# An exponential's table loaded one slot earlier, a freer choice of slots for side work, and two sums issued with their product, in a kernel that runs TensorE from end to end

## The chip, the cores and the metric

The kernel runs on one core of a Trainium2 chip. The metric is device time in microseconds (us), the median over several executions. One execution is also recorded by the hardware profiler; the times inside it are counted from the start of its span.

## The reference

Two mixers of the same input `x` (2048 tokens of 1024) are blended token by token by a gate. `a` is attention with 32 heads of 32, in which every token looks at 8 tokens at distances 0, 2, ... 14; `b` is a gated MLP whose gate half is normalised and mixed along the sequence by the 2048 x 2048 matrix `w_sp`.

```
g   = sigmoid((x * gate_w).sum(-1))
qkv = x @ wqkv                                  # 1024 -> 3 x 1024, 32 heads
attn = softmax(q . k[pos - 2w] * scale), w = 0..7   # masked where pos - 2w < 0
a   = (attn . v[pos - 2w]) @ wo
z   = gelu(x @ w_in)                            # 1024 -> 2 x 1792
b   = (z1 * (w_sp @ layernorm(z2) + b_sp)) @ w_out
out = g * a + (1 - g) * b
```

## The kernel before

All products run on TensorE, most of them by a Strassen-like scheme: one block product is made of seven half-size products (`a11`, `s1`, `s2`, `a12`, `s3`, `s4`, `a22`) that share PSUM banks. A bank that has been read out by a copy is added to by later products, so a product into it has to wait for the copy. The scheme works with 16-bit floats, for which operands are scaled by powers of two; the powers come from sums of magnitudes that are taken beside the other work.

The stages, by the profile's clock: projections to z2 and to the first heads' q, k, v (to 92 us, with x turned round and scaled); projections of two groups of heads with z2's last columns in between, as eight **projection groups** (`z2_group`, 92 to 182 us); the last three groups of heads and the rest of z2 (to 270 us); z1 (to 362 us); the **mixing** along the sequence, sixteen groups (`g_group`, n = 0 to 15, 362 to 532 us); the product with wo; the product with w_out (580 us to the end).

The attention itself runs on VectorE beside all of this, from 92 to about 497 us: for each of eight groups of heads a product of q with k (L505), folds of it (L509, L512), the maximum and its subtraction (`soft_a`, L526 to L529), the exponential on ScalarE (L552), the sum and division (`soft_b`, L556 to L562), a product with v (L572) and its folds (L578, L579, L575).

Every engine runs its instructions in the order in which they are written. That order is made when the kernel is built, by a planner, `Beat`. It keeps a clock `beat.now` that advances by the columns of the matmuls as they are written (`beat.run`), a list of steps with due times (`beat.at`), and an estimate of when VectorE is free (`beat.vector`, pushed on by `on_vector`). Whenever `beat.run` advances, it writes all steps that have fallen due, the attention's among them. In the projection groups an attention step is written when its start is at most 0.3 us ahead, in the mixing at most 0.5.

In a projection group the products `s1`, `s3` and `s4` go to the banks `pd`, `pa` and `pd`, tiles of q, k, v (L938, copied out by ACT at L941) lie between, and two sums (L486, L487) put the group's last two blocks together on VectorE. The second of them reads the bank `pd`, which frees it.

A mixing group writes its seven products and, on ScalarE, in this order: a copy of `pa` into a second bank (the *fork*, L1130), a *fork slot* for side work, the copies `p5` (L1116) and `u2` (L1118), the first block's copy from `pb` (L1152), a *copy slot* for side work, the copy `u3` (L1118), two passes of magnitudes of the group before (L885), and the last block's copy (L1168). In every odd group from 3 on, both slots are taken by the scaling of an earlier unit (L903). In the others side work may take them, from two lists of steps with due times:

- `beside_fork`, for the fork slot, holds the pass over o's magnitudes (`o_norm_now`, L681, 1.9 us). What has not been done by the time VectorE is to write over `o`'s buffer is written there and then, by the attention's own product (`pv_steps`).
- `beside_copy`, for the copy slot, holds first a tiny exponential (L1193) that only makes the table be loaded, and then seven passes over chunks of A_wo (`wo_norm`, L858, 768 columns each). All chunks use one buffer: each pass, when it is written, plans the load of the next chunk (L854) for 1 us later.

ScalarE holds one table of functions at a time. The mixing's first exponential follows GELUs, so a table load precedes whichever exponential comes first. All loads and stores are issued by SyncE (SP), in one order.

Of the kernel before, what the change touches and what calls it, by code (L numbers as in the profile page):

```python
# [35 lines left out]
DN = ZC + 2  # L36
# [26 lines left out]
def kernel(  # L63
# [13 lines left out]
    nc = tc.nc  # L77
# [67 lines left out]
    wsc = sm.tile([P, 4], F32, name="wsc")  # L145
# [11 lines left out]
    cm05 = sm.tile([P, 8], F32, name="cm05")  # L157
# [22 lines left out]
    m11, m12, m21, m22 = [d_h[:, q] for q in range(4)]  # L180
# [159 lines left out]
    beat = Beat()  # L340
# [6 lines left out]
    TT = nc.vector.tensor_tensor  # L347
# [30 lines left out]
    def z2_out(src, i, c, scale):  # L378
        nc.scalar.activation(z2[:, i, ZC * c:ZC * (c + 1)], src, ACT.Gelu_apprx_tanh, scale=scale,
                             accum_out=s1[:, 4 * i + c:4 * i + c + 1])  # L380
# [61 lines left out]
    def z2_keep(ps):  # L442
        out = z2_snaps[z2_kept[0] % 5]
        z2_kept[0] += 1
        nc.scalar.copy(out, ps[:, 0:DN - 1])
        return out

    def z2_product(ps, w, v, first):
        for k in range(4):
            lhsT = w[:, k // 2, k % 2, :] if len(w.shape) == 4 else w[:, k, :]  # L450
            nc.tensor.matmul(ps[:, 0:DN - 1], lhsT, v[:, k, 0:DN - 1], start=(first and k == 0), stop=(k == 3),  # L451
                             skip_group_check=True)
        beat.run(4 * (DN - 1))

    def z2_late(i, src, scale):
        z2_out(src[:, 0:ZC], i, 3, scale)
        nc.scalar.activation(gl_s[:, i:i + 1], src[:, ZC:ZC + 1], ACT.Copy, scale=scale)
# [3 lines left out]
    def z2_group(u, tiles):  # L461
        v = tokens[u]
        scale = zinv
        pa, pd = [psum.tile([P, 512], F32, name="ps", tag="ps") for _ in range(2)]
        z2_product(pa, v.a11, m11, True)
        pb = seeded.tile([P, 512], F32, name="seed", tag="sd")
        nc.scalar.copy(pb[:, 0:DN - 1], pa[:, 0:DN - 1])
        tiles.pop(0)()
        z2_product(pd, v.s1, r1, True)
        p5 = z2_keep(pd)  # L470
        z2_product(pa, v.s2, r2, False)
        u2 = z2_keep(pa)
        tiles.pop(0)()
        while z2_wait:
            z2_late(*z2_wait.pop(0))
        z2_product(pb, v.a12, m21, False)
        z2_out(pb[:, 0:ZC], 2 * u, 2, scale)
        z2_product(pa, v.s3, r3, False)
        u3 = z2_keep(pa)
        tiles.pop(0)()  # L480
        prep["owed"] += 2 if 0 < u < 5 else 0
        some = release()
        if not some:
            square_owed(u)
        z2_product(pd, v.s4, m22, False)
        TT(p5, p5, u3, ALU.add)  # L486
        TT(u2, u2, pd[:, 0:DN - 1], ALU.add)  # L487
        beat.on_vector(1.3)
        z2_product(pa, v.a22, r4, False)
        z2_out(pa[:, 0:ZC], 2 * u + 1, 2, scale)  # L490
        tiles.pop(0)()
        if not release(True) and not some and u % 2 == 1:
            square_owed(u)
        z2_wait.extend([(2 * u + 1, p5, scale), (2 * u, u2, scale)])
# [44 lines left out]
    def release(last=False):  # L539
        for fn in list(held):  # L540
            if not (last and fn is exp_now):
                held.remove(fn)
                fn()
                return True
        return False
# [49 lines left out]
    def load_v(g):  # L595
        sync.dma_start(v_t, bass.AP(tensor=v_d.tensor, offset=v_d.offset + (g * (S + 16) + 2) * C, ap=[[NJ * C, P], [1, NJJ * C]]))
# [5 lines left out]
    def attention_steps(t):  # L602
        ready = t
        beat.at(t - 8.0, lambda: load_qk(0))
        beat.at(t - 7.9, lambda: load_v(0))
        for g in range(NG):
            if g == 1:
                t = max(t, ready + 28.0)
            for took, fn in qk_steps(0) + qk_steps(1):
                yield t, took, fn  # L610
            t = beat.vector
            if g + 1 < NG:
                beat.at(t + 1.0, lambda g=g: load_qk(g + 1))
            if g > 0:
                for took, fn in pv_steps(g - 1, 0):
                    yield t, took, fn
                t = beat.vector
            yield t + (0.5 if g == 0 else 0.0), 1.7, soft_a
            t = beat.vector
            exp_wait.append(g)  # L620
            beat.at(t + 1.0, lambda: hold_back(exp_now))
            if g == 0:
                t += 5.0
            else:
                for took, fn in pv_steps(g - 1, 1):
                    yield t, took, fn
                t = beat.vector
                beat.at(t + 1.0, lambda g=g: load_v(g))
                beat.at(t + 1.5, lambda g=g: store_o(g - 1))
                o_wait.append(lambda g=g: o_norm(g - 1, obuf))  # L630
                if prep["mixing"]:
                    beside_fork.append((t + 12.0, o_norm_now))
                else:
                    beat.at(t + 17.0, o_norm_soon)
            yield t, 2.3, lambda g=g: soft_b(g)
            t = beat.vector
        for took, fn in pv_steps(NG - 1, 0) + pv_steps(NG - 1, 1):
            yield t + 5.0, took, fn
        t = beat.vector
        beat.at(t + 1.0, attended)  # L640

    beside_fork, beside_copy, behind_mult = [], [], []
# [5 lines left out]
            room[0] -= behind_mult[0][1]  # L648
            behind_mult.pop(0)[2]()

    def spare(queue):
        if queue and queue[0][0] <= beat.now:
            queue.pop(0)[1]()

    def attended():
        store_o(NG - 1)
# [195 lines left out]
    def load_wo_chunk(m):  # L852
        n = min(768, 8192 - 768 * m)
        sync.dma_start(w_chunk[:, 0:n], wo_flat[:, 768 * m:768 * m + n])  # L854

    def wo_norm(m):
        n = min(768, 8192 - 768 * m)
        nc.scalar.activation(w_chunk[:, 0:n], w_chunk[:, 0:n], ACT.Abs, accum_out=l1[:, m:m + 1])  # L858
        if m < 10:
            beat.at(beat.now + 1.0, lambda: load_wo_chunk(m + 1))  # L860

    def w_total():
        nc.vector.memset(zeros[:], 1.0)
# [136 lines left out]
    def square_owed(u):  # L1000
        if prep["owed"] > 0:
            prep["owed"] -= 1
            squares(u)
            return True
# [35 lines left out]
    t = beat.now  # L1040
# [18 lines left out]
    t = beat.now  # L1059
# [4 lines left out]
    t = beat.now  # L1064
# [13 lines left out]
    for c in range(4):  # L1078
        w1 = w1_slots[c]
        for i in range(16):  # L1080
# [5 lines left out]
            ps = bank()  # L1086
# [46 lines left out]
    def g_group(n):  # L1133
        u, fb = n // 2, n % 2
        f0, f1 = fb * ZC, fb * ZC + ZC
        v = pairs[u % 2]
        lo, hi = [bt[:, 2 * u + h:2 * u + h + 1] for h in range(2)]
        g, z = g_ring[n % 4], z1_ring[n % 2]
        now(("z1", n), ("y", u - 2))
        pa, pd = [psum.tile([P, 512], F32, name="ps", tag="ps") for _ in range(2)]  # L1140
        product(pa, v.a11, b11, f0, f1, True)
        pb = fork(pa, ZC, lo)
        if n % 2 == 1 and n > 1:
            y_scale_beside((n - 3) // 2, 0)
        else:
            spare(beside_fork)
        product(pd, v.s1, t1, f0, f1, True)
        p5 = keep(pd, None)
        product(pa, v.s2, t2, f0, f1, False)
        u2 = keep(pa, lo)  # L1150
        product(pb, v.a12, b21, f0, f1, False)
        nc.scalar.copy(g[:, 0, 0], pb[:, 0:ZC])  # L1152
        if n % 2 == 1 and n > 1:
            y_scale_beside((n - 3) // 2, 1)
        else:
            spare(beside_copy)
        idle_vector()
        product(pa, v.s3, t3, f0, f1, False)
        u3 = keep(pa, hi)
        if n > 0:  # L1160
            y_norm(n - 1)
        vec(g[:, 1, 1], p5, u3)
        product(pd, v.s4, b22, f0, f1, False)
        vec(g[:, 0, 1], pd[:, 0:ZC], u2)
        if fb == 0 and n > 0:
            y_power(n // 2 - 1)
        product(pa, v.a22, t4, f0, f1, False)
        nc.scalar.activation(g[:, 1, 0], pa[:, 0:ZC], ACT.Identity, bias=hi)  # L1168
        TT(g, g, z, ALU.mult)
        beat.on_vector(1.1)  # L1170
        room[0] = 7.0 if fb == 1 else 6.5 if n == 14 else 1.5
        idle_vector()
        if n + 2 < 2 * NU:
            soon(("z1", n + 2), lambda: load_z1(n + 2))
# [15 lines left out]

    for n in range(2):
        load_z1(n)
    beside_copy.append((0.0, lambda: nc.scalar.activation(wsc[:, 3:4], cm05[:, 0:1], ACT.Exp)))  # L1193
    for m in range(4, 11):
        beside_copy.append((beat.now + 1.0, lambda m=m: wo_norm(m)))
    behind_mult.append((beat.now + 134.0, 0.5, w_total))
# [1 line left out]
    for n in range(2 * NU):  # L1198
        u, fb = n // 2, n % 2
        t = beat.now  # L1200
# [21 lines left out]
    t = beat.now  # L1222
# [110 lines left out]
    for u in range(NU):  # L1333
        v = rows[u % 5]
        lo, hi = [omr[:, 2 * u + h:2 * u + h + 1] for h in range(2)]
        m11, m12, m21, m22 = halves(u, mix)
        o11, o12, o21, o22 = halves(u, ob_slots)
        pa, pd = [psum.tile([P, 512], F32, name="ps", tag="ps") for _ in range(2)]
# [6 lines left out]
        p5 = hold(pd, hi)  # L1345
        product(pa, v.s2, e2, 0, 512, False)
        u2 = hold(pa, lo)
# [4 lines left out]
        u3 = hold(pa, hi)  # L1352
# [53 lines left out]
```

## Time and profile before

| What | us |
|---|---|
| median of 3 runs (672.32 to 672.66) | 672.64 |
| the profiled execution | 671.37 |
| its span | 669.6 |
| TensorE busy in the span | 663.5 |
| VectorE busy | 575.2 |
| ScalarE busy | 441.6 |
| DMA: moved, mean share of the 16 engines | 123.92 MB, 69.8% |
| mixing, 362 to 532: TensorE, VectorE, ScalarE busy of 170 | 169.25, 155.72, 120.05 |

In the profile PE is TensorE's matmuls, PEld its weight loads, DVE is VectorE, ACT ScalarE, SP the engine that issues the DMAs. Busy time counts an instruction from start to end. The ends of matmuls are modelled, so that gaps between matmuls are better read from their starts. A row of the timeline merges instructions of one kind that follow each other, and its bracket gives the idle time of the engine just before and what ended it. Idle time of an engine matters only where TensorE, or whatever runs last, waits for it.

### The profile page before, as it was taken

The page shows a single profiled execution, that of the slowest core. Times are in us where ns is not written, and L with a number is a line of the kernel's source. Part 1 is how long each engine was busy: PE and PEld are TensorE (multiplying, and loading weights), DVE is VectorE, ACT ScalarE, POOL GpSimd, SP SyncE. Part 2 cuts the span into 40 slices and gives each one's busy share as a digit, 9 for nine tenths or more (in the row PEclk, how much of TensorE's full clock was granted, in tenths as well). Part 3 has the DMA queues.
Part 4 walks back from the last instruction along what each step waited for, and adds up shares of the span by engine and source line. Part 5 has one row for each costly group of instructions (what it writes and reads, how often), then busy time and mean ns, then how long its engine had stood idle before and what let it go on. Part 6 is the DMA issues. An engine that isn't in the chain of part 4 may idle for free.

```text
span 669.6 us, 9598 instructions
## 1 busy us (share of the span) xinstructions
PE 663.5 (99%) x3564; PEld 389.8 (58%) x3564; DVE 575.2 (86%) x660; ACT 441.6 (66%) x774; POOL 9.4 (1%) x68
## 2 busy tenths in 40 slices
PE   9999999999999999999999999999999999999998
PEld 4568876666777777555555455555555544444443
DVE  4667999989999999999999999999978788954745
ACT  4437667788889989889754568777777774522122
POOL 0000000000001000000000000000000000000000
PEclk9999999999999999999999999999999999999999
DMA  8999574354298996994956686648589799476211
GB/s 237 176 246 269 103 203 131 91 121 119 49 278 250 281 303 186 277 342 146 276 209 217 140 216 162 159 123 231 141 209 287 144 242 253 93 159 150 56 63 64
DMA packets 229919, 123.92 MB, mean 185 GB/s; under 512 B 191088, under 2 KB 217456, under 8 KB 229872
## 3 DMA queue, kind: packets, MB, share of 16 engines
q1 hardware_dynamic: 229872, 123.31, 69.8%
q8 instruction: 28, 0.46, 0.3%
q14 instruction: 19, 0.16, 0.1%
HBM read 63.97 MB, written 37.82 MB: 152 GB/s over the span
## 4 chain that ended last, share of the span: by engine, by line
PE 55%; DVE 40%; ACT 3%; issue 2%; DVEq 0%; ACTq 0%
PE ps L1106 36%; DVE arena L509 8%; DVE arena L505 7%; DVE arena L572 7%; PE seed L1106 6%; PE ps L938 6%; DVE arena L578 3%; PE ps L370 2%; DVE arena L801 2%; PE sd L938 2%; DVE arena L579 2%; DVE arena L819 2%; DVE arena L575 1%; DVE att_L L512 1%; PE sd L370 1%
## 5 line engine op out<-in xcount | busy, mean ns | idle before, releaser
L1106 PE MATMUL ps<-arena 128*128 128x448 f16 (+1 forms) x1296 | 263.7, 363 | 0.7 <-ACT arena L1118 0.6
L1106 PEld LDWEIGHTS <-arena 128*128 128x128 f16 x1519 | 148.5, 98 | 155.0 <-issue 1.5
L938 PEld LDWEIGHTS <-arena 128*128 128x128 f16 (+1 forms) x1024 | 141.4, 138 | 30.6 <-issue 1.1
L938 PE MATMUL ps<-arena 128*128 128x384 bf16 x800 | 142.5, 326 | 0.7 <-DVE arena L487 0.7
L1089 PEld LDWEIGHTS <-arena 128*128 128x128 f16 x512 | 50.0, 98 | 46.6
L509 DVE TENSOR_TENSOR arena<-arena 128x4096 bf16<-128x4096 bf16 (+1 forms) x64 | 74.0, 1157 | 1.8
L1089 PE MATMUL ps<-arena 128*128 128x448 bf16 x384 | 75.4, 352 | 0.0
L505 DVE TENSOR_TENSOR arena<-arena 128x8192 bf16<-128x8192 bf16 x16 | 70.8, 4422 | 4.4 <-DMA arena<-k_d 4.1
L572 DVE TENSOR_TENSOR arena<-arena,att_A 128x8192 bf16<-128x8192 bf16 x16 | 70.7, 4420 | 0.2
L941 ACT CAST arena<-ps 128x384 bf16<-128x384 f32 x100 | 47.8, 487 | 29.4 <-PE ps L938 28.7
L1106 PE MATMUL seed<-arena 128*128 128x448 f16 (+2 forms) x223 | 48.7, 360 | 0.0
L370 PE MATMUL ps<-arena 128*128 128x448 bf16 x216 | 45.4, 352 | 0.2 <-ACT arena L355 0.2
L451 PE MATMUL ps<-arena 128*128 128x449 f16 x192 | 42.3, 353 | 0.0
L938 PE MATMUL sd<-arena 128*128 128x384 bf16 x224 | 41.0, 326 | 0.0
L1092 ACT ACTIVATE arena<-ps,x_sc 128x448 bf16<-128x448 f32 x48 | 29.5, 639 | 15.5 <-PE ps L1089 11.9
L1330 ACT ACTIVATE arena<-ps,omr 128x512 f32<-128x512 f32 x24 | 16.5, 687 | 32.7 <-PE ps L1106 32.7
L370 PEld LDWEIGHTS <-arena 128*128 128x128 f16 (+1 forms) x256 | 24.9, 98 | 22.0 <-ACT arena L355 0.5
L578 DVE TENSOR_TENSOR arena<-arena 128x4096 bf16<-128x4096 bf16 x16 | 36.6, 2287 | 0.2
L1264 DVE SCALAR_TENSOR_TENSOR arena<-seed,omr,arena 128x512 bf16<-128x512 f32 x8 | 6.0, 751 | 32.7 <-PE seed L1106 32.7
L451 PEld LDWEIGHTS <-arena 128*128 128x128 f16 x224 | 21.9, 98 | 18.1 <-issue 0.5
L760 ACT ACTIVATE arena<-arena 128x2048 bf16<-128x2048 bf16 x16 | 30.9, 1929 | 0.0
L885 ACT ACTIVATE arena<-arena 128x896 bf16<-128x896 bf16 x32 | 30.3, 947 | 0.5
(190 smaller groups left out, 738.4 us busy)
## 6 DMA issues: line engine op xcount, KB each, us to landing
arena<-in_B_w_sp_dram SPq DMA_DIRECT2D x16, 512.0 KB, 4.1
arena<-v_d SPq DMA_DIRECT2D x8, 960.0 KB, 6.6
z_d<-arena SPq DMA_DIRECT2D x16, 448.0 KB, 4.5
arena<-z_d SPq DMA_DIRECT2D x16, 448.0 KB, 3.6
y_d<-arena SPq DMA_DIRECT2D x16, 448.0 KB, 3.0
arena<-k_d SPq DMA_DIRECT2D x7, 960.0 KB, 7.3
arena<-in_A_wqkv_dram SPq DMA_DIRECT2D x24, 256.0 KB, 4.7
q_d<-arena SPq DMA_DIRECT2D x32, 128.0 KB, 2.5
```

What stands on the lines that cost most here:

```text
L370: nc.tensor.matmul(ps[:, 0:N], x[:, kt, i * P:(i + 1) * P], _sub_ap(w2, kt * W2P + ZC * c, [[1, N]]), start=(kt == 0), stop=(kt == KT - 1) ...
L451: nc.tensor.matmul(ps[:, 0:DN - 1], lhsT, v[:, k, 0:DN - 1], start=(first and k == 0), stop=(k == 3), skip_group_check=True)
L505: TT(prod.rearrange("p (w j c) -> p w j c", w=W, j=8, c=C), in0, in1, ALU.mult)
L509: return lambda: TT(pv[:, :, 0:n], pv[:, :, 0:n], pv[:, :, n:2 * n], ALU.add)
L572: TT(prod.rearrange("p (w j d h) -> p w j d h", w=W, j=8, d=DH, h=HG), in0, in1, ALU.mult)
L578: return [(4.4, mul), (2.3, lambda: TT(p3[:, 0:4, :], p3[:, 0:4, :], p3[:, 4:8, :], ALU.add)), (1.2, lambda: TT(p3[:, 0:2, :], p3[:, 0:2, ...
L760: nc.scalar.activation(slot, slot, ACT.Abs, accum_out=l1[:, a:a + 1])
L885: nc.scalar.activation(waste, g_ring[n % 4][:, r], ACT.Abs, accum_out=yl[:, k:k + 1])
L938: nc.tensor.matmul(ps[:, 0:3 * C].rearrange("p (t c) -> p t c", t=3), lhsT, wgt[:, :, kt, :], start=(kt == 0), stop=(kt == KT - 1))
L941: nc.scalar.copy(st[:, j % 4, :].rearrange("p (t d h) -> p t d h", t=3, h=HG), ps[:, 0:3 * C].rearrange("p (t h d) -> p t d h", t=3, h=HG))
L1089: nc.tensor.matmul(ps[:, 0:512 if whole and kt == 0 else ZC], xh[:, kt, i * P:(i + 1) * P], _sub_ap(w1, kt * ZC, [[1, 512 if whole and kt ...
L1106: nc.tensor.matmul(ps[:, 0:c1 - c0], w[:, k, :], v[:, k, c0:c1], start=(first and k == 0), stop=(k == K - 1), skip_group_check=True)
```

## The change

Five edits, all to the order in which work is written; no operation is added or taken away, and no matmul moves.

1. The tiny exponential that makes the table be loaded moves from the head of the copy slot's list to the head of the fork slot's.
2. Either slot of a mixing group may take work from either list, the fork slot's list first (`spare` with both).
3. The pass over o's magnitudes falls due 6 us, not 12, after the attention's products in the mixing.
4. A pass over a chunk of A_wo puts the next pass off until 9 us later.
5. In a projection group the two sums are written right after the four matmuls of `s4`, before the planner's clock advances over them, instead of after it.

```diff
-    def z2_product(ps, w, v, first):
+    def z2_product(ps, w, v, first, then=()):
         for k in range(4):
...
+        for fn in then:
+            fn()
         beat.run(4 * (DN - 1))
...
-        z2_product(pd, v.s4, m22, False)
-        TT(p5, p5, u3, ALU.add)
-        TT(u2, u2, pd[:, 0:DN - 1], ALU.add)
-        beat.on_vector(1.3)
+        z2_product(pd, v.s4, m22, False, (lambda: TT(p5, p5, u3, ALU.add),
+                                          lambda: TT(u2, u2, pd[:, 0:DN - 1], ALU.add),
+                                          lambda: beat.on_vector(1.3)))
...
-                    beside_fork.append((t + 12.0, o_norm_now))
+                    beside_fork.append((t + 6.0, o_norm_now))
...
-    def spare(queue):
-        if queue and queue[0][0] <= beat.now:
-            queue.pop(0)[1]()
+    def spare(*queues):
+        for queue in queues:
+            if queue and queue[0][0] <= beat.now:
+                queue.pop(0)[1]()
+                return
...
         if m < 10:
             beat.at(beat.now + 1.0, lambda: load_wo_chunk(m + 1))
+        if beside_copy:
+            beside_copy[0] = (beat.now + 9.0, beside_copy[0][1])
...
-            spare(beside_fork)
+            spare(beside_fork, beside_copy)
...
-            spare(beside_copy)
+            spare(beside_fork, beside_copy)
...
-    beside_copy.append((0.0, lambda: nc.scalar.activation(wsc[:, 3:4], cm05[:, 0:1], ACT.Exp)))
+    beside_fork.insert(0, (0.0, lambda: nc.scalar.activation(wsc[:, 3:4], cm05[:, 0:1], ACT.Exp)))
```

## The prediction

> **What bounds the kernel now.** I read the page first, then the waits of TensorE, then the timeline around each of those waits, and last the order of instructions on each engine of the changed kernel as built against that of before. The page says who sets the end:
>
> ```profile
> PE 663.5 (99%) x3564; PEld 389.8 (58%) x3564; DVE 575.2 (86%) x660; ACT 441.6 (66%) x774; POOL 9.4 (1%) x68
> PEclk9999999999999999999999999999999999999999
> ```
>
> TensorE is busy from end to end at the full granted clock, and the change alters no matmul (the order on PE is the same row for row). So it can only win or lose what TensorE waits. The waits of PE (engine and line, who released it, us in total, times, longest):
>
> ```profile
> PE pw L114 <- DVE arena L109: 1.2, 1, 1.2
> PE ps L938 <- DVE arena L487: 0.7, 2, 0.5
> PE ps L1106 <- ACT arena L1118: 0.6, 1, 0.6
> PE ps L370 <- ACT arena L355: 0.2, 1, 0.2
> PE ps L1106 <- ACT seed L1130: 0.2, 1, 0.2
> ```
>
> The ends of matmuls are modelled, so I count a stall from starts: 48 matmuls take 9.08 us in the chain of waits, 0.189 us each. Three places matter, one for each part of the change. The timeline of mixing group 0 (start us, duration us, engine, line, what, count, idle before and its releaser):
>
> ```profile
> 364.21 0.61 ACT L1130 ACTIVATE seed<-ps,bt 128x448 f32<-128x448 f32 x1 [0.88 <-PE ps L1106]
> ...
> 365.66 0.53 ACT L1116 COPY arena<-ps 128x448 f32<-128x448 f32 x1 [0.84 <-PE ps L1106]
> ...
> 367.18 0.63 ACT L1118 ACTIVATE arena<-ps,bt 128x448 f32<-128x448 f32 x1 [0.98 <-PE ps L1106]
> ...
> 368.49 3.19 PE L1106 MATMUL ps<-arena 128*128 128x448 f16 x16
> ...
> 369.13 1.28 ACT L552 ACT_TABLE_LOAD   x1 [1.32 <-DVE att_L L529]
> 370.43 0.72 ACT L552 ACTIVATE att_L<-att_L,x_sc 128x512 f32<-128x512 f32 x1
> 371.06 0.51 ACT L1152 CAST arena<-seed 128x448 bf16<-128x448 f32 x1
> 371.47 0.20 ACT L1193 ACTIVATE wsc<-cm 128x1 f32<-128x1 f32 x1
> 371.57 0.62 ACT L1118 ACTIVATE arena<-ps,bt 128x448 f32<-128x448 f32 x1
> 372.25 6.21 PE L1106 MATMUL ps<-arena 128*128 128x448 f16 x32 [0.57 <-ACT arena L1118]
> ```
>
> The 16 matmuls from 368.49 are done issuing at 368.49 + 16 x 0.189 = 371.52; the next, into the same bank, waits for the last copy out of it (L1118, `u3`) until 372.25. 0.73 us are lost, because ACT loaded the exponential's table between the subtraction of L529 and the exponential, with four ACT operations queued behind. The end of mixing group 9, which began at 458.50, and that of projection group 2 (the view is the timeline again):
>
> ```profile
> 469.41 1.89 ACT L681 ACTIVATE arena<-arena 128x2048 bf16<-128x2048 bf16 x1
> ...
> 471.82 0.59 ACT L1130 ACTIVATE seed<-ps,bt 128x448 f32<-128x448 f32 x1
> ...
> 472.46 1.67 PE L1106 MATMUL ps<-arena 128*128 128x448 f16 x8 [0.18 <-ACT seed L1130]
> ```
>
> ```profile
> 123.58 4.42 DVE L572 TENSOR_TENSOR arena<-arena,att_A 128x8192 bf16<-128x8192 bf16 x1
> ...
> 128.45 0.62 DVE L487 TENSOR_TENSOR arena<-arena,ps 128x449 f32<-128x449 f32 x1
> ...
> 129.12 1.46 PE L938 MATMUL ps<-arena 128*128 128x384 bf16 x8 [0.47 <-DVE arena L487]
> ```
>
> In the first, o's magnitudes (L681) stand ahead of the fork L1130; 40 matmuls from 464.56 end at 472.12, so 0.34 us are lost. In the second, the two sums stand behind a 4.42 us product of the attention; eight matmuls from 126.96 end at 128.48, so 0.64 us are lost, and at 107.25 us, with L505 ahead, 0.38 (105.35 + 8 x 0.19 = 106.87).
>
> **The two sums.** In the built order they move only in projection groups 4, 5 and 6: ahead of one 0.4 us fold (L509), of another, and of one L575 (0.69 us). The stalls lie after groups 0 and 2, and there the order is unchanged, because the 4.42 us product was already queued before the product `s4`. In groups 4 to 6 the sums start now at 148.68, 159.31 and 169.55, and TensorE had begun the next group at 146.85, 157.42 and 167.98: the inputs were long there, so the sums run at once, the fold is 1.07 us later, and whatever follows both (L512, L526) starts when it did. No stall of PE is listed there. Cost 0, gain 0; the cover is that DVE's sum of work is unchanged, and without it each group could lose at most those 0.4 to 0.7 us of DVE, which nobody waits for.
>
> **o's magnitudes.** The due time t + 6 in place of t + 12 and the second slot should free the place at 469 us. In the built order they stay in the fork slot of mixing group 4 and, pulled in by the attention's next product, behind the two magnitude passes (L885) of groups 9 and 12, exactly as before. The 0.34 us stay. Gain 0.
>
> **A_wo's magnitudes** (L858, 0.85 us and 0.19 for its accumulator). Seven of them stood in the copy slots of groups 1, 2, 4, 6, 8, 10 and 12. They now stand in the copy slots of 0, 1, 2, 4 and 10 and the fork slots of 6 and 8. A fork slot has carried 1.79 us (L903) without a stall, so 6 and 8 cost nothing; 12 becomes free, where PE did not wait either. Each issues the load of the next chunk (L854, 0.35 us of SP), which moves with it: in groups 0, 6 and 8 it now stands ahead of a load of z1 (L834). In group 0 SP was idle from 373.09 to 377.87 there, and z1 lands 3.4 to 5.6 us after its issue for a group 10 us on. Nothing.
>
> **The table** is the part on the path. Behind the fork (ends 364.82) the load takes 1.28 and the small exponential 0.20, so L1116 moves from 365.66 to about 366.2 and ends at 366.7. Its bank `pd` is written again only at 370.00, and `u2` at 367.18 is gated by TensorE as before: hidden, with 3.3 us to spare. Then the exponential starts at 369.13 itself. By pitches of the rows: to L1152 0.63 (370.43 to 371.06), so 369.76; to a chunk of A_wo, new here, 0.43 (380.01 to 380.44 in group 1), so 370.19; to its accumulator 0.74 (380.44 to 381.18), so 370.93; to the next operation 0.09 (471.21 to 471.30) or at most 0.34 (381.18 to 381.52, where it may have waited for PE), so L1118 runs from 371.02 to 371.27 at its start and ends 371.64 to 371.89; PE follows 0.06 later (372.19 to 372.25), at 371.70 to 371.95. Against 371.52 it loses 0.18 to 0.43 where it lost 0.73: a gain of 0.30 to 0.55, and 0.73 if the chunk costs nothing. I take 0.5, near the 0.09 pitch, since in that place `pa` is finished at 370.2 and nothing but ACT's own queue is left. What is late next is still L1118, by the chunk put ahead of it.
>
> The Trainium skill speaks against the fork slot (ScalarE: Activation LUTs, What ACT_TABLE_LOAD costs): a switch of table costs about 1283 ns and a drain of about 1380 ns. The trace has 1.28 for the load; the load at 134.20 us starts 0.02 after the copy before it and its exponential 0.01 after it, so no drain shows. By that rule `u2` would end at about 368.74 and the gain be 0.42 in place of 0.5.
>
> **The sum.** The profiled execution took 671.37 us, 669.6 of span and 1.77 around it; it lies 1.27 under the median of the runs, 672.64. 671.37 - 0.5 = 670.87 for such an execution, and 672.64 - 0.5 = 672.1 for the median, 0.08% less. A difference of 0.2%, about what a measurement of this kernel can tell from no change, is 1.35 us; all the stalls named above, 0.73 + 0.34 + 0.64 + 0.38, are 2.1.
>
> **Rivals.** (1) Slower: a late chunk. In group 1 the chunk pass is now one load further on, and its load (chunk 5) can go out only behind the two transposes that hold SP from 368.06 to 373.09; before, it had gone from 381.40 for group 2. ACT would stop in the copy slot of group 1 until it lands, with `u3` behind it and TensorE behind that. TensorE needs its bank at 379.81 + 16 x 0.189 - 0.5 = 382.3, so the chunk has to land by 380.8, 7.7 us after its issue; from 8.2 us on all the gain is lost. For it: one such load (issued at 333.16, behind four rearranging copies) took 11.6 us, and ACT stood 5.7 us for it. As long here, it lands at 384.7, PE restarts at 386.2, and the time is 672.1 + 3.9 = 676.0. Against it: the median of these loads is 3.1 us, and the transposes ahead land in 4.6. Chance 0.11. (2) Given back: the chunk in group 0 delays L1118 as much as the table did (from 0.55 us more than the pitches say). 672.6, chance 0.08; the pitches speak against it. (3) Faster: the sums also cure the stalls after groups 0 and 2, 0.64 + 0.38 more, 671.1. The built order speaks against it; with what the spread of the runs (0.34) can add to a full 0.73 and a lost 0.34, chance 0.08. (4) ACT has to run dry before a load of a table, which at 369.13 would have lain in the 1.32 us that it stood idle anyway: at most 1.32. Then L1116 starts at 364.82 + 1.32 + 1.28 + 0.10 = 367.52, `u2` 0.53 later at 368.05, ending 368.68, and PE restarts at 368.74 in place of 368.49: 0.25 lost there, and none at L1118, which is then waited for no more (due at 371.77, free at 371.70). 672.64 - 0.73 + 0.25 = 672.2. Chance 0.03.
>
> **How the numbers follow.** My forecast, 0.70. Its own range: gain 0 to 0.73, and 0.34 of spread to either side, 671.6 to 673.0. I add 0.2 below, if part of the 0.34 us at 472 goes as well, and 0.1 above for a mild case of (1): 671.4 to 673.1. That leaves out (1) and (3), 0.19. Within 0.2%: 0.70 + 0.08 + 0.03 = 0.81; faster 0.08; slower 0.11.
>
> **What would show it.** Right: a table load at about 364.8 between L1130 and L1116, an exponential straight behind L529, a chunk pass at about 370.2, the wait of PE for L1118 (0.6) gone or 0.2 to 0.4 by starts, and the other PE waits (0.7 for the sums twice, 0.2 for the fork) still there at 107, 129 and 472 us. Wrong: a second wait of the chunk pass for its DMA, a PE wait in group 1, or sums that no longer hold PE at 129 us.

## The result: 0.15% faster, and the profile after

The changed kernel takes 671.63 us (median of 22 runs) against 672.65 (22 runs): ratio 0.9985, interval 0.9978 to 0.9991, that is 1.0 us less, somewhere between 0.6 and 1.5. The profiled execution took 671.09, its span is 669.3.

In the changed kernel's file the line numbers are shifted: L1118 is L1123, L1130 is L1135, L1116 is L1121, L552 is L553, L529 is L530, L487 is L488, L572 is L573, L858 is L861. The waits of PE (us in total, times, longest):

```profile
PE pw L114 <- DVE arena L109: 1.2, 1, 1.2
PE ps L943 <- DVE arena L488: 1.0, 2, 0.6
PE ps L370 <- ACT arena L355: 0.3, 1, 0.3
PE ps L1111 <- ACT seed L1135: 0.2, 1, 0.2
```

The wait for `u3` (L1118, 0.6) is gone; those for the sums and for the fork are there as before. The timeline of mixing group 0:

```profile
364.63 0.61 ACT L1135 ACTIVATE seed<-ps,bt 128x448 f32<-128x448 f32 x1 [0.88 <-PE ps L1111]
365.25 1.28 ACT L1198 ACT_TABLE_LOAD   x1
...
366.55 0.20 ACT L1198 ACTIVATE wsc<-cm 128x1 f32<-128x1 f32 x1
366.66 0.51 ACT L1121 COPY arena<-ps 128x448 f32<-128x448 f32 x1
...
367.59 0.63 ACT L1123 ACTIVATE arena<-ps,bt 128x448 f32<-128x448 f32 x1 [0.42 <-PE ps L1111]
...
368.90 9.24 PE L1111 MATMUL ps<-arena 128*128 128x448 f16 x48
...
369.38 0.72 ACT L553 ACTIVATE att_L<-att_L,x_sc 128x512 f32<-128x512 f32 x1 [1.16 <-DVE att_L L530]
370.01 0.51 ACT L1157 CAST arena<-seed 128x448 bf16<-128x448 f32 x1
370.42 0.84 ACT L861 ACTIVATE arena<-arena 128x768 bf16<-128x768 bf16 x1
371.17 0.19 ACT L861 ACTIVATION_READ_ACCUMULATOR arena<-arena 128x1 f32 x1
371.26 0.62 ACT L1123 ACTIVATE arena<-ps,bt 128x448 f32<-128x448 f32 x1
```

The load lies behind the fork, `u2` (367.59) is again gated by TensorE, the exponential stands straight behind L530, and `u3` ends at 371.88, just ahead of the 368.90 + 16 x 0.189 = 371.92 at which TensorE wants its bank. So 48 matmuls stand in one unbroken row, where before there were 16 and a gap.

The two profiled executions differ by only 0.28 us, less than the medians. The reason shows when the same matmul is found in each trace: all kernels here issue the same 3564 matmuls in the same order, so a stretch between the starts of two of them can be compared. I cut at the matmuls that follow the waits of before: the one after projection group 0's sums (107 us), after group 3 (139), the last product of mixing group 0 (372), and the one behind mixing group 9's fork (472). The first stretch begins with the first matmul (1.18 us), the last ends with the start of the last one. The rows e0 to e11 are the experiments below; e4, e5, e7 and e9 to e11 were executed once each, so that for them the stretches speak and the time alone does not.

| kernel (us) | start to 107 | 107 to 139 | 139 to 372 | 372 to 472 | 472 to end |
|---|---|---|---|---|---|
| before | 106.07 | 31.87 | 233.13 | 100.22 | 193.57 |
| before, again (e0) | 107.39 | 31.86 | 233.13 | 100.22 | 193.56 |
| changed | 106.49 | 31.86 | 232.40 | 100.22 | 193.56 |
| table alone (e1) | 107.81 | 31.86 | 232.57 | 100.21 | 193.56 |
| sums alone (e2) | 106.35 | 31.87 | 232.93 | 100.22 | 193.56 |
| slots alone (e3) | 107.16 | 31.87 | 233.12 | 100.22 | 193.56 |
| o late (e4) | 106.36 | 31.87 | 232.42 | 99.88 | 193.57 |
| three tables (e5) | 106.35 | 31.86 | 234.28 | 100.22 | 193.56 |
| sums first (e7) | 106.26 | 31.25 | 232.40 | 100.22 | 193.56 |
| all (e8) | 106.56 | 31.24 | 232.40 | 99.88 | 193.57 |
| sums in 6 (e9) | 106.29 | 31.87 | 232.91 | 100.22 | 193.56 |
| sums in 4, 5 (e10) | 106.50 | 31.86 | 233.11 | 100.22 | 193.56 |
| exponential behind u3 (e11) | 106.87 | 31.86 | 232.40 | 100.22 | 193.56 |

From 107 us on, a stretch that an edit leaves alone repeats to about 0.02 us; the first column alone scatters, by 1.7 us between 106.07 and 107.81. The change took 0.73 us, all of it between 139 and 372. The profiled pair hides that, since the changed one's first stretch was 0.42 longer.

The traces also tell what the first column hangs on. The attention's first product of q with k waits for k's load to land, 4.1 us in the kernel before and 5.5 in e1:

```profile
55.55 4.42 DVE L505 TENSOR_TENSOR arena<-arena 128x8192 bf16<-128x8192 bf16 x1 [4.10 <-DMA arena<-k_d]
```

```profile
57.29 4.42 DVE L505 TENSOR_TENSOR arena<-arena 128x8192 bf16<-128x8192 bf16 x1 [5.51 <-DMA arena<-k_d]
```

In all eleven traces in which the sums of projection group 0 stand behind an attention product, the matmul after them starts 51.69 to 51.71 us after that row (55.55 to 107.25, 57.29 to 108.99). So the landing of one load sets the length of the first stretch. It is not the change's doing: on every engine, the two kernels hold the same instructions in the same order up to 148 us.

### The profile page after: what moved, and what is told of

Read it like the earlier page. It is cut to its first block, busy times and chain, and to the rows that moved or that the text cites. A ratio compares the mean times of both kernels' runs of the same rounds, so it can differ in the third digit from the quotient of the medians.

```text
span 669.3 us, 9594 instructions
## 1 busy us (share of the span) xinstructions
PE 663.3 (99%) x3564; PEld 389.5 (58%) x3564; DVE 575.0 (86%) x660; ACT 441.9 (66%) x774; POOL 9.4 (1%) x68
## 4 chain that ended last, share of the span: by engine, by line
PE 92%; DVE 6%; ACT 1%; DMA 0%; issue 0%; ACTq 0%
PE ps L1111 38%; PE ps L943 17%; PE ps L1094 11%; PE seed L1111 7%; PE ps L370 6%; PE sd L943 5%; PE sd L1094 4%; PE ps L451 3%; DVE arena L510 1%; DVE arena L506 1%; DVE arena L573 1%; PE sd L370 1%; PE seed L451 1%; PE pw L114 0%; DVE arena L579 0%; DMA q_d<-arena 0%
## 5 line engine op out<-in xcount | busy, mean ns | idle before, releaser
L573 DVE TENSOR_TENSOR arena<-arena,att_A 128x8192 bf16<-128x8192 bf16 x16 | 70.7, 4421 | 0.2
L579 DVE TENSOR_TENSOR arena<-arena 128x4096 bf16<-128x4096 bf16 x16 | 36.6, 2288 | 0.2
```

Of the source, the lines that this page charges most:

```text
L573: TT(prod.rearrange("p (w j d h) -> p w j d h", w=W, j=8, d=DH, h=HG), in0, in1, ALU.mult)
L579: return [(4.4, mul), (2.3, lambda: TT(p3[:, 0:4, :], p3[:, 0:4, :], p3[:, 4:8, :], ALU.add)), (1.2, lambda: TT(p3[:, 0:2, :], p3[:, 0:2, ...
```

## The experiments

**e0, the kernel before again.** No edit.

> The kernel before, unchanged, timed against itself: what a comparison of this size can tell, and a second profile of it. Theory A (the table alone makes the gain, and the stall at L1118 in mixing group 0 differs from execution to execution with VectorE's lead or lag on TensorE): ratio 1.000 within 0.1%, and in this profile the lost time by starts in mixing group 0 is not 0.73 us again but anywhere from 0.4 to 1.5. Theory B (the stall is fixed, and the other half of the gain comes from the sums): ratio 1.000, lost time 0.7 to 0.75 again.

Measured: 672.75 us (11 runs), ratio 0.9995, interval 0.9986 to 1.0004. So a comparison of 11 runs tells nothing under 0.1%. The lost time in mixing group 0 was 0.73 again, to the hundredth, which is against theory A: the stall is the same each time, whatever the first stretch was. Where VectorE and TensorE are brought into step is told with e7.

**e1, the table alone.**

```diff
-    beside_copy.append((0.0, lambda: nc.scalar.activation(wsc[:, 3:4], cm05[:, 0:1], ACT.Exp)))
+    beside_fork.insert(0, (0.0, lambda: nc.scalar.activation(wsc[:, 3:4], cm05[:, 0:1], ACT.Exp)))
```

> The kernel before with the table's exponential at the head of the fork slot's list and nothing else. Theory A: the whole gain, 0.9 to 1.1 us (ratio 0.9985), no PE wait for the copy u3 in mixing group 0. Theory B: half of it, 0.4 to 0.6 us (ratio 0.9992).

Measured: ratio 0.9991, interval 0.9981 to 1.0001, which fits both. The stretch decides: 232.57, that is 0.56 gained and 0.17 still lost, with the table load where it was meant to be and the chunk's pass behind the exponential. Timeline of e1, mixing group 0:

```profile
370.23 6.01 PE L1106 MATMUL ps<-arena 128*128 128x448 f16 x30
370.88 0.72 ACT L552 ACTIVATE att_L<-att_L,x_sc 128x512 f32<-128x512 f32 x1 [1.33 <-DVE att_L L529]
371.51 0.51 ACT L1152 CAST arena<-seed 128x448 bf16<-128x448 f32 x1
371.92 0.84 ACT L858 ACTIVATE arena<-arena 128x768 bf16<-128x768 bf16 x1
372.66 0.19 ACT L858 ACTIVATION_READ_ACCUMULATOR arena<-arena 128x1 f32 x1
372.75 0.62 ACT L1118 ACTIVATE arena<-ps,bt 128x448 f32<-128x448 f32 x1
```

`u3` ends at 373.37, TensorE wanted its bank at 370.23 + 3.03 = 373.26. The wait is too short for the bracket of a row or for the view of waits; it shows in starts only.

**e2, the sums alone.** The two hunks of `z2_product` and `z2_group`, nothing else.

> The kernel before with the two sums written ahead of the planner's advance and nothing else. Theory A: no gain (ratio 1.000), the PE waits for the second sum (0.7 us, twice) still there. Theory B: 0.4 to 0.6 us gained (ratio 0.9992).

Measured: ratio 0.9989, interval 0.9981 to 0.9998; the stretch 232.93, 0.20 gained. Both PE waits for the sums are still there (0.8 in two). The stretch decides again, since the interval takes in 0.1 to 1.3 us. Theory B was right that the sums have a part, and wrong in its size; A was wrong on the gain and right on the waits.

**e3, the slots alone.** `spare` over both lists, t + 6, the 9 us, and the table's exponential held for the copy slot:

```diff
-    beside_copy.append((0.0, lambda: nc.scalar.activation(wsc[:, 3:4], cm05[:, 0:1], ACT.Exp)))
+    beside_copy.append((beat.now + 3.0, lambda: nc.scalar.activation(wsc[:, 3:4], cm05[:, 0:1], ACT.Exp)))
```

> The kernel before with either slot open to either list, the due times of the change, and the table's exponential held in the copy slot of group 0, so that the table is still loaded in front of the attention's exponential. Theories A and B: no gain (ratio 1.000) and a PE wait for the copy u3 in group 0 of about 0.6 us. Theory C (the chunks' passes in fork slots are what helps): 0.4 to 1.0 us gained.

Measured: ratio 0.9998, interval 0.9988 to 1.0008; stretch 233.12 and the PE wait for `u3` 0.6. Theory C falls: by the stretches, these edits alone are worth nothing.

**e9 and e10, where the 0.20 of the sums is.** The kernel before, with the sums written early in projection group 6 alone, and in 4 and 5 alone (in e10 the line with `early` has `(4, 5)`):

```diff
-        z2_product(pd, v.s4, m22, False)
-        TT(p5, p5, u3, ALU.add)
-        TT(u2, u2, pd[:, 0:DN - 1], ALU.add)
-        beat.on_vector(1.3)
+        sums = (lambda: TT(p5, p5, u3, ALU.add), lambda: TT(u2, u2, pd[:, 0:DN - 1], ALU.add),
+                lambda: beat.on_vector(1.3))
+        early = u in (6,)
+        z2_product(pd, v.s4, m22, False, sums if early else ())
+        for fn in () if early else sums:
+            fn()
```

> The kernel before with the two sums written early in projection group 6 alone. Theory (there the sums come between a fold of VectorE and the next fold, which reads its result, and fill the time that the second would have waited): all of the 0.20 us of the sums' part is here; TensorE's stretch from projection group 3 to mixing group 0's last copy is 232.93 us, against 233.13 before. Rival (it comes from groups 4 and 5): 233.13.

> The kernel before with the two sums written early in projection groups 4 and 5 alone. Theory: no gain, since there the sums separate one dependent pair of folds and join another as close: the same stretch is 233.13 us. Rival: 232.93.

Measured: 232.91 and 233.11. It is group 6, as expected. Timeline of DVE there, before:

```profile
167.61 1.23 DVE L579 TENSOR_TENSOR arena<-arena 128x2048 bf16<-128x2048 bf16 x1
168.94 0.69 DVE L575 TENSOR_TENSOR arena<-arena 128x1024 bf16<-128x1024 bf16 x1
169.55 0.62 DVE L486 TENSOR_TENSOR arena<-arena 128x449 f32<-128x449 f32 x1
170.09 0.62 DVE L487 TENSOR_TENSOR arena<-arena,ps 128x449 f32<-128x449 f32 x1
170.62 0.42 DVE L526 TENSOR_TENSOR att_m<-att_L 128x256 f32<-128x256 f32 x1
```

and in e2 (L579 and L575 are L580 and L576, the sums L487 and L488, L526 is L527):

```profile
167.90 1.23 DVE L580 TENSOR_TENSOR arena<-arena 128x2048 bf16<-128x2048 bf16 x1
169.04 0.62 DVE L487 TENSOR_TENSOR arena<-arena 128x449 f32<-128x449 f32 x1
169.58 0.61 DVE L488 TENSOR_TENSOR arena<-arena,ps 128x449 f32<-128x449 f32 x1
170.12 0.68 DVE L576 TENSOR_TENSOR arena<-arena 128x1024 bf16<-128x1024 bf16 x1
170.72 0.42 DVE L527 TENSOR_TENSOR att_m<-att_L 128x256 f32<-128x256 f32 x1
```

The same five instructions take 3.01 us to the start of the last (167.61 to 170.62) before and 2.82 (167.90 to 170.72) after. L575 reads what L579 wrote and starts 1.33 after it; a sum, which does not, starts 1.14 after it, while L579 is still listed as busy. Of these 0.19, 0.07 belong to this one place: of the sixteen L575, three have a wait for a semaphore of their own in front, this one among them, and where L575 follows L579 without one it starts 1.26 after it (121.32 and 132.56 us). Instructions of L575 before, and in e9 (where it is L579), where the one at 168.9 is gone:

```profile
L575 DVEq EVENT_SEMAPHORE  x3: 21/21/21, 168.9 to 366.7; - x3
```

```profile
L579 DVEq EVENT_SEMAPHORE  x2: 21/21/21, 258.1 to 366.7; - x2
```

The 0.19 lasts to mixing group 0, because VectorE is never idle for more than 0.11 us at a time from 136 us to L529 at 368. Counted from TensorE's matmul at 139, L529 there starts at 229.25 before, 229.23 in e10 and 229.03 in e9. ACT comes earlier to its exponential by as much, and `u3` to its end.

**e11, another cure.** The kernel before, with the attention's exponential written behind `u3` in the mixing, and none of the change's edits:

```diff
-        if prep["groups"]:
+        if prep["groups"] or prep["mixing"]:
             held.append(fn)
...
         u3 = keep(pa, hi)
+        release()
```

> The kernel before with one edit that the change does not have: in the mixing the attention's exponential is written behind the copy u3, and the table is loaded in group 0's copy slot. Theory (it was the exponential with its table ahead of u3 that held TensorE, and nothing waits for the exponential soon): the lost time in mixing group 0 is 0, the stretch 232.40 us, as in the changed kernel, with none of its edits. Rival (the table in the copy slot still holds u3): 0.1 to 0.7 us lost.

Measured: 232.40, nothing lost, though the table is now loaded in the copy slot ahead of `u3`. Timeline of e11:

```profile
370.02 1.28 ACT L1194 ACT_TABLE_LOAD   x1
371.31 0.20 ACT L1194 ACTIVATE wsc<-cm 128x1 f32<-128x1 f32 x1
371.42 0.62 ACT L1118 ACTIVATE arena<-ps,bt 128x448 f32<-128x448 f32 x1
371.94 0.71 ACT L552 ACTIVATE att_L<-att_L,x_sc 128x512 f32<-128x512 f32 x1
```

`u3` ends at 372.04, ahead of TensorE's next product (372.31). So one table load ahead of `u3` is affordable here. What was not is a table load that could not start before VectorE's subtraction, with the exponential and the cast between it and `u3`.

**e5, three tables in the fork slot.** The changed kernel with more of the disputed cost:

```diff
-    beside_fork.insert(0, (0.0, lambda: nc.scalar.activation(wsc[:, 3:4], cm05[:, 0:1], ACT.Exp)))
+    def tables():
+        for f in (ACT.Exp, ACT.Gelu_apprx_tanh, ACT.Exp):
+            nc.scalar.activation(wsc[:, 3:4], cm05[:, 0:1], f)
+
+    beside_fork.insert(0, (0.0, tables))
```

> The changed kernel with three table loads and three small functions in the fork slot of group 0 instead of one (exponential, GELU, exponential). Theory (a load costs 1.28 us and nothing more, hidden until u2 is late): ACT is busy there for 3 x 1.41 = 4.2 us from 365.25, u2 ends at about 370.6 by the changed kernel's clock and TensorE's third product starts 1.8 us late; nothing more is lost at u3. Rival (each load also costs a drain of over a microsecond): 3 to 6 us lost.

Measured: 1.88 us lost, at the third product only (stretch 234.28 = 232.40 + 1.88). Timeline of e5:

```profile
365.11 1.28 ACT L1200 ACT_TABLE_LOAD   x1
366.40 0.20 ACT L1200 ACTIVATE wsc<-cm 128x1 f32<-128x1 f32 x1
366.62 1.28 ACT L1200 ACT_TABLE_LOAD   x1
...
369.95 0.64 ACT L1123 ACTIVATE arena<-ps,bt 128x448 f32<-128x448 f32 x1
...
370.64 3.56 PE L1111 MATMUL ps<-arena 128*128 128x448 f16 x18 [1.72 <-ACT arena L1123]
```

A load with its small function takes 1.51 us (365.11 to 366.62), with 0.02 or less on either side of the 1.28; three take 4.43. No drain of over a microsecond shows, contrary to the figure of the Trainium skill (ScalarE: Activation LUTs, What ACT_TABLE_LOAD costs). Two more loads with their functions put 3.03 us (365.11 to 368.14) ahead of `u2` and cost 1.88, so behind one load `u2` had 1.15 to spare. A second load, 1.51, would by this estimate make it 0.36 late: one is what the slot holds.

**e4, o's magnitudes in the fork slot of group 10.** The changed kernel with

```diff
         def mul():
-            if jh == 0:
-                o_norm_now()
...
         def last():
+            if jh == 0:
+                o_norm_now()
```

> The changed kernel with the pass over o's magnitudes no longer written with the attention's product but, if no slot has taken it by then, with the last fold that overwrites o's buffer; it then goes to the fork slot of mixing group 10. Theory (the pass stands in the way of the fork at the end of group 9): the lost time there falls from 0.34 us to 0, and the stretch of TensorE from the matmul after mixing group 0's last copy to the one after that fork falls from 100.22 to 99.88 us; all other stretches as in the changed kernel. Rival (the fork was held by the scaling passes ahead, not by this one): 0.34 us stay.

Measured: 99.88 and a loss of 0, as expected. The fork no longer waits for the pass (L684 here), which now stands behind it:

```profile
470.39 0.61 ACT L1135 ACTIVATE seed<-ps,bt 128x448 f32<-128x448 f32 x1 [0.79 <-PE ps L1111]
470.92 1.90 ACT L684 ACTIVATE arena<-arena 128x2048 bf16<-128x2048 bf16 x1
```

The pass that the change meant to move, and did not, was worth 0.34 us.

**e7, the sums of groups 0 to 2 ahead of the 4.42 us products.** The changed kernel; steps that fall due are kept back in these groups until the sums are written:

```diff
-                    fn()
+                    if self.kept is None:
+                        fn()
+                    else:
+                        self.kept.append(fn)
...
+        if u == 0:
+            beat.kept = []
+        if u == 1:
+            beat.kept = []
         z2_product(pa, v.s3, r3, False)
+        if u == 2:
+            beat.kept = []
         u3 = z2_keep(pa)
...
+        kept, beat.kept = beat.kept or [], None
+        for fn in kept:
+            fn()
         z2_product(pa, v.a22, r4, False)
```

> The changed kernel with the sums of projection groups 0, 1 and 2 written ahead of the attention's 4.42 us product that stood before them. Theory (VectorE's chain, not TensorE, sets when mixing group 0 can finish, because its exponential waits for a subtraction on VectorE): the PE waits for the second sum at 107 and 129 us go (0.62 us at 129 and what 107 has), but the loss at mixing group 0 comes back, at 0.6 to 1.3 us, so that the end is where the changed kernel has it within 0.3 us. Rival: the 1.0 us are gained in full.

Measured: both PE waits gone (31.25, 0.61 less, and no wait at 107), and the loss at mixing group 0 did not come back: 232.40. My theory was wrong here and the rival right. At 107 the gain is an estimate, 0.86: with the 51.70 us of the other traces behind its first product of q with k (56.60), the matmul would have started at 108.30, and it did at 107.44. VectorE does not run on its own clock from 107 to 369 us: after projection group 2 it stands idle until ACT delivers an exponential that has its place behind a copy from TensorE. Its row there, before and then in e7 (L556 is L570, L552 is L566):

```profile
136.26 0.43 DVE L556 TENSOR_TENSOR att_m<-att_L 128x256 f32<-128x256 f32 x1 [3.00 <-ACT att_L L552]
```

```profile
135.83 0.43 DVE L570 TENSOR_TENSOR att_m<-att_L 128x256 f32<-128x256 f32 x1 [1.39 <-ACT att_L L566]
```

In that idle time it catches up with a TensorE that comes earlier. This wait, 1.2 to 3.0 us in all thirteen traces, brings the two engines into step; behind it VectorE has no room left, which is why the stall in mixing group 0 repeats to the hundredth.

**e8, all of it.** e7 with the edits of e4 and e11.

> The changed kernel with the sums of projection groups 0 to 2 ahead of the attention's product, o's magnitudes in group 10's fork slot, and the attention's exponential behind the copy u3 in the mixing. Theory: TensorE no longer waits at 129 (0.62), at 472 (0.34) or in mixing group 0; 1.0 to 1.7 us faster than the changed kernel, 2 to 2.7 faster than before (ratio about 0.9965). Rival (the waits only move on to the next work that VectorE delivers): no more than 0.34 us faster than the changed kernel, ratio 0.998.

Measured: 670.25 us (5 runs), ratio to before 0.9965, interval 0.9951 to 0.9979, as expected. Its stretches are those of e4 and e7 together: from 107 us on, 0.96 less than the changed kernel (0.62 and 0.34), beside what the wait at 107 was. It was not timed side by side with the changed kernel. The exponential's place adds nothing to e7 and e4: 232.40 was reached without it.

## Why the prediction was right, and where it was not

**The place and the mechanism** were right: 0.73 us were lost in mixing group 0, and the table's load, hidden behind the fork, took 0.56 of them away (e1, e5). The other 0.17 went with the sums.

**The size.** 0.5 was forecast, 0.73 is in the stretches, 1.0 in the medians with 0.6 to 1.5 as interval. The term of the table alone was 0.30 to 0.55 with 0.5 taken; it measured 0.56, with a pitch of 0.09 from the chunk's accumulator to `u3` (372.66 to 372.75). What the medians have beyond 0.73 is within their interval, and no edit is shown to have made it.

**The term that failed** is that of the sums, cost 0 and gain 0. The step that whatever follows both starts when it did holds in groups 4 and 5 (e10) and not in 6, where it starts 0.19 earlier (e9). I had taken an instruction's pitch as its own, where it depends on what stands in front. The cover failed too, that nobody waits for those 0.4 to 0.7 us of VectorE: the exponential of mixing group 0 waits for L529, as a row of the prediction shows, and on its way there VectorE is never idle for more than 0.11 us at a time (e9, e10). 0.56 and 0.20 are 0.76, of which 0.73 were there to be won.

**What else was read rightly.** The built order told that the sums would not cure the waits at 107 and 129, that o's magnitudes would stay, and that the slots would bring nothing (e3). The 3.3 us to spare for the load behind the fork held for the bank `pd` alone; `u2` had 1.15 (e5).

**The rivals.** The late chunk did not happen: its load went out at 373.27, as expected behind the transposes, and its pass in group 1 began at 380.13 without waiting; the chunks' only wait for a DMA is still the one in z1's stage (4.2 us). The chunk in group 0 gave back 0.17 of the table's gain, and the sums paid for it. The fork slot needed no empty ACT ahead of a load (e5).

**The range** held partly by luck. The mechanism's own lowest time was 672.64 - 0.73 = 671.9, and 671.63 is below it; it is inside only because I gave the runs 0.34 of spread, taken from three of them. Over 22 runs the changed kernel went from 670.6 to 673.5. In the profiled executions such scatter is that of the first stretch; for the other runs no trace shows it.

## What to carry to other kernels

Where the busiest engine never idles, find each of its gaps by starts and ask what stood in the queue of the engine it waited for: 0.73 us were lost behind a table load that could as well have run in a slot in which its engine was idle. An engine that is idle nowhere on its way to that queue hands on every 0.1 us that it is spared. A built order tells which waits an edit can't touch, before anything runs. And when runs scatter more than the effect, compare stretches between the same instructions of two traces: here they repeat to 0.02 us where medians of eleven runs could not tell 0.1%.

## What the runs showed of the hardware that was not expected

A VectorE instruction that does not read its predecessor's result starts while that one is still listed as busy (1.14 us after a 1.23 us fold). One that does starts 0.03 after its end (1.26 after the same fold), and 0.10 after it where it also had a semaphore's wait of its own in front (1.33). So reordering five instructions without removing any gained 0.19 us. Table loads in a row cost 1.51 and 1.52 us each with a 128x1 function between them, with no gap over 0.02 us on either side of the load (e5).
